# A fused attention and two-MoE kernel: blocks of four token tiles, a planner that models the VectorE/GpSimd port and two DMA rings, and new ranks

## The chip, the cores and the metric

One core of one Trainium2 chip runs the whole program. The metric is the device time of one execution in microseconds (us). The kernel before has a median of 745.53 us in three runs (744.16 to 746.38).

## The reference

Three layers follow each other, all in fp32.

- Clustered attention, batch 2, 8 heads, 768 tokens, head size 64. Queries and keys are assigned to the nearest of 16 centroids of their head (argmax of normalised products); a query sees only the keys of its own cluster: `scores = where(q_assign == k_assign, q @ k.T / 8, -1e9)`, softmax, `attn @ v`.
- First MoE layer on 1536 tokens of 512: `h = x @ w_in` (512 to 1024), `solu = h * softmax(h)`, layer norm over the 1024 with gain `g_ln`, `@ w_out` (1024 to 512).
- Second MoE layer: `((x @ w_a) * (x @ w_b)) @ w_out2`, 512 to 1536 to 512.

## The kernel before, in words

Every matmul operand is kept as two fp32r halves, `hi` (the rounded value) and `lo` (the rest), and a product is three matmuls (hi hi, hi lo, lo hi). ScalarE or GpSimd writes `hi` with a cast, VectorE or GpSimd writes `lo` with a subtraction. Weights arrive as 64-bit words of doubles; `weight()` turns each piece of 512 KB into fp32 with shifts and masks (lines 560 to 582) and then into two halves (591 and `sub`, 467 or 469).

Attention works on 8 pairs of heads. A pair is loaded and transposed (`qk_part`), compared with the centroids (`do_sim`, `do_sims`), turned into one-hot rows (`do_arg`, `do_oh`), and placed by DMA from SBUF to SBUF beside q and k (`do_place`, `do_ohd`), so that one extra matmul adds the mask. Then 96 steps of 128 queries follow: `score` (959), maximum (963), exp (967), `turn` (transposes 991, halves 1008 and 469), `apply` (1023 and after). The last part of `apply` writes the two halves of the layer's output into a common space of 12,288 columns, x.

The first MoE goes by 12 token tiles of 128: `moe_h` (1146), `moe_ln` (1163 to 1194), `moe_lnt` (1218), and, for each group of two tiles, `moe_x2` (1235, evictions 1249), which writes the new x in the place of the old.

The second MoE is cut into units. A unit is one block of token tiles and one of 12 slices of 128 hidden columns. `moe2_ab` multiplies the slice of `w_b` and of `w_a` with the block (1294, 12 matmuls each, the block's tokens as the moving columns), copies, multiplies and splits the result (1305 to 1308), and `moe2_y` multiplies it by the slice of `w_out2` (1322), three matmuls of 512 columns for each tile, adding up in PSUM over six slices. After the first six slices of a block the sum is put aside, after the last six it is added (1342) and sent out. A block has BT = 3 tiles, so BN = 384 moving columns, and there are 4 blocks. x is laid out by block: `[block][half][chunk of 128 inputs][384 tokens]`.

Nothing runs in the order in which it is written. `pl.add(engine, cost, rank, ...)` notes an operation with its buffers; `Plan.schedule` then simulates all engines, lets each take, of what is ready, the operation of the lowest rank, and emits the instructions in that order. Each engine then works in its order, held by semaphores. An operation's rank is a formula of its place plus corrections from the table `ADJ`, by kind, engine and number. SyncE issues all DMAs, and the planner gives a transfer a cost on one ring.

Of the kernel before, what the change touches and what calls it, by code (L numbers as in the profile page):

```python
# [33 lines left out]
ADJ = {  # L34
# [1374 lines left out]
```

## Time and profile before

| | us |
|---|---|
| median of three runs | 745.53 |
| the profiled execution | 743.77 |
| its span, first to last instruction | 742.0 |
| PE (TensorE matmul) busy | 711.1 |
| DVE (VectorE) busy | 473.7 |
| ACT (ScalarE) busy | 397.7 |
| POOL (GpSimd) busy | 339.5 |

The profile is of one execution. Engines are named as in the table; PEld is TensorE's weight load, which overlaps PE; SP is SyncE. Busy time counts instructions, not waiting, and the ends of matmuls are modelled. A group of instructions is shown with its line, engine, operation, `out<-in`, shapes and count. The chain of waits is followed back from the last instruction to what released it. Transfers moved 60.74 MB at a mean of 82 GB/s.

### The profile page before, as it was taken

The page shows a single profiled execution, that of the slowest core. Times are in us where ns is not written, and L with a number is a line of the kernel's source. Part 1 is how long each engine was busy: PE and PEld are TensorE (multiplying, and loading weights), DVE is VectorE, ACT ScalarE, POOL GpSimd, SP SyncE. Part 2 cuts the span into 40 slices and gives each one's busy share as a digit, 9 for nine tenths or more (in the row PEclk, how much of TensorE's full clock was granted, in tenths as well). Part 3 has the DMA queues.
Part 4 walks back from the last instruction along what each step waited for, and adds up shares of the span by engine and source line. Part 5 has one row for each costly group of instructions (what it writes and reads, how often), then busy time and mean ns, then how long its engine had stood idle before and what let it go on. Part 6 is the DMA issues. An engine that isn't in the chain of part 4 may idle for free.

```text
span 742.0 us, 12400 instructions
## 1 busy us (share of the span) xinstructions
PE 711.1 (96%) x4441; PEld 653.9 (88%) x4441; DVE 473.7 (64%) x866; ACT 397.7 (54%) x870; POOL 339.5 (46%) x429
## 2 busy tenths in 40 slices
PE   6889999999999999799999999999999999999997
PEld 6779888899999987678898999999999999999996
DVE  6899898988889878999688537763134311112122
ACT  4788899899899985564344424442224211211110
POOL 6568898857856425465515527771036300000000
PEclk9799999999999999999999999999999999999999
DMA  8878644454534001222301303431002000101011
GB/s 225 199 167 199 167 104 137 114 138 118 125 75 112 12 1 57 85 86 86 111 33 57 110 5 114 134 122 57 1 28 87 29 1 1 42 1 43 1 42 43
DMA packets 40573, 60.74 MB, mean 82 GB/s; under 512 B 3896, under 2 KB 35392, under 8 KB 40512
## 3 DMA queue, kind: packets, MB, share of 16 engines
q1 hardware_dynamic: 40512, 59.95, 29.0%
q8 instruction: 35, 0.57, 0.3%
q14 instruction: 26, 0.21, 0.1%
HBM read 36.74 MB, written 3.15 MB: 54 GB/s over the span
## 4 chain that ended last, share of the span: by engine, by line
PE 69%; DVE 18%; ACT 6%; issue 4%; POOL 2%; DMA 0%; DVEq 0%; ACTq 0%; POOLq 0%
PE psT L1294 12%; PE psS L1322 12%; PE psO L1023 6%; PE psM L1294 6%; PE psO L1294 6%; PE psT L991 6%; PE psS L959 6%; PE psS L1146 3%; PE psM L1235 3%; PE psO L1235 3%; DVE R L469 3%; DVE F L578 2%; DVE mxn L963 2%; DVE F L567 2%; ACT R L1008 1%
## 5 line engine op out<-in xcount | busy, mean ns | idle before, releaser
L469 DVE TENSOR_TENSOR R<-psT,R 128x384 fp32r<-128x384 f32 (+1 forms) x216 | 119.0, 565 | 26.9 <-ACT R L1008 23.3
L467 POOL TENSOR_TENSOR R<-F,R 128x512 fp32r<-128x512 f32 (+2 forms) x84 | 89.5, 1071 | 85.8 <-ACT R L591 81.7
L1294 PE MATMUL psT<-R 128*128 128x384 f32 x576 | 108.3, 337 | 0.0
L1322 PE MATMUL psS<-R 128*128 128x512 f32 x432 | 107.2, 393 | 0.2 <-ACT F L1340 0.2
L1294 PEld LDWEIGHTS psT<-R 128*128 128x128 f32 x576 | 102.1, 188 | 3.8
L991 PE MATMUL psT<-ident,F 128*128 128x128 f32 x576 | 92.8, 276 | 5.0 <-DVE R L469 4.4
L1008 ACT CAST R<-psT 128x384 fp32r<-128x384 f32 x192 | 90.1, 483 | 11.0 <-PE psT L991 8.8
L1322 PEld LDWEIGHTS psS<-R 128*128 128x128 f32 x432 | 80.2, 188 | 15.4 <-ACT F L1340 0.5
L1023 PE MATMUL psO<-R 128*128 128x256 f32 x576 | 91.0, 294 | 2.2 <-ACT F L1043 2.0
L959 PE MATMUL psS<-R 128*128 128x512 f32 (+3 forms) x384 | 92.2, 363 | 0.6 <-ACT F L967 0.6
L963 DVE TENSOR_REDUCE mxn<-psS 128x1 f32<-128x768 f32 x96 | 91.1, 948 | 2.0 <-PE psS L959 1.7
L967 ACT ACTIVATE F<-psS,mxn 128x768 f32<-128x768 f32 x96 | 87.5, 911 | 2.7 <-DVE mxn L963 2.4
L1307 ACT CAST R<-F 128x384 fp32r<-128x384 f32 x48 | 24.7, 515 | 102.6 <-PE psS L1322 100.6
L582 POOL TENSOR_TENSOR F<-F 128x512 int32<-128x512 int32 x45 | 60.2, 1339 | 41.6 <-DVE F L578 38.2
L1023 PEld LDWEIGHTS psO<-R 128*128 128x128 f32 x576 | 74.7, 189 | 4.1 <-ACT F L1043 3.3
L1308 DVE TENSOR_TENSOR R<-F,R 128x384 fp32r<-128x384 f32 x48 | 31.9, 664 | 70.6 <-ACT R L1307 70.5
L991 PEld LDWEIGHTS psT<-ident,F 128*128 128x128 f32 x576 | 66.5, 140 | 11.4 <-DVE R L469 8.0
L959 PEld LDWEIGHTS psS<-R 128*128 128x128 f32 (+1 forms) x384 | 66.8, 194 | 10.3 <-ACT F L967 1.5
L1146 PE MATMUL psS<-R 128*128 128x512 f32 x288 | 69.5, 394 | 1.5 <-DVE F L1167 1.2
L1146 PEld LDWEIGHTS psS<-R 128*128 128x128 f32 x288 | 52.9, 188 | 12.6 <-DVE F L1167 1.7
L1305 ACT COPY F<-psT 128x384 f32<-128x384 f32 x48 | 23.0, 479 | 60.5 <-PE psT L1294 59.5
L591 ACT CAST R<-F 128x512 fp32r<-128x512 f32 x52 | 32.2, 619 | 41.0 <-POOL F L582 33.2
(139 smaller groups left out, 1152.7 us busy)
## 6 DMA issues: line engine op xcount, KB each, us to landing
F<-in_moe_w_out_dram SPq DMA_DIRECT2D x20, 512.0 KB, 3.2
R<-R SPq DMA_DIRECT2D x32, 288.0 KB, 4.8
R<-R SPq DMA_DIRECT2D x32, 192.0 KB, 4.8
F<-in_moe_w_b_dram SPq DMA_DIRECT2D x12, 512.0 KB, 3.5
F<-in_moe_w_a_dram SPq DMA_DIRECT2D x12, 512.0 KB, 3.4
F<-in_moe_w_in_dram SPq DMA_DIRECT2D x8, 512.0 KB, 6.7
F<-in_v_dram SPq DMA_DIRECT2D x8, 384.0 KB, 3.3
R<-R SPq DMA_DIRECT2D x30, 96.0 KB, 2.7
```

Source lines behind the costliest of these rows:

```text
L467: pl.add("POOL", pool(n), rank, lambda: G.tensor_tensor(out=out_, in0=in0, in1=in1, op=ALU.subtract), reads, writes)
L469: pl.add("DVE", dve(n), rank, lambda: V.tensor_tensor(out=out_, in0=in0, in1=in1, op=ALU.subtract), reads, writes)
L582: pl.add("POOL", pool(n), rank, lambda: G.tensor_tensor(out=u, in0=u, in1=low, op=ALU.add), [rk, lwk], [uk])
L959: T.matmul(sp[:, c0:c0 + cn], kq[:r, 2 * m, t * P:(t + 1) * P], kq[:r, 2 * m + 1, c0:c0 + cn], start=m == 0, stop=m == 1)
L963: pl.add("DVE", dve(S), i + SUB["max"], lambda: V.tensor_reduce(out=mxn[:, b:b + 1], in_=sp[:, :S], axis=AX.X, op=ALU.max, negate=True), [ ...
L967: pl.add("ACT", act(S) + 93 + 93, i + SUB["exp"], lambda: A.activation(F[:, po:po + 768], sp[:, :S], AF.Exp, bias=mxn[:, b:b + 1], scale=1 ...
L991: T.transpose(sp[:, c, :], pt[:, kt * P:(kt + 1) * P], ident)
L1008: pl.add("ACT", act(HN), rk, lambda sp=sp, dh=dh: A.copy(dh, sp), [sk], [hk])
L1023: T.matmul(psO[:, :GN], vs[:, kt, j].rearrange("p l d -> p (l d)"), pt[:, m, kt, :], start=(kt == 0 and m == 0), stop=(kt == NT - 1 and m ...
L1146: T.matmul(sp[:, n0:n0 + 512], xb[:, a, c, ts_], winv[:, w, c, n0:n0 + 512], start=first, stop=(c == KD - 1 and a == 1))
L1294: T.matmul(pt[:, :BN], w[:, l, c, :], xb[:, a, c, :], start=first, stop=(c == KD - 1 and l == 1))
L1322: T.matmul(yv[t][0], hl2[a][:, ts_], wo[:, l, :], start=(first and a == 0 and l == 0), stop=(last and a == 1))
```

## The change

Five things change; the arithmetic does not.

- The planner's model. An operation can be marked `port=True` (VectorE steps that read and write SBUF with two ports); these and all GpSimd operations take turns at one port. A transfer is a pair of KB for two rings, each at 200 GB/s, and the ninth transfer waits for the first. `dma()` takes KB in place of nanoseconds; a plain transfer is split evenly, a placement goes by one ring.
- All ranks in `ADJ` have new values (669 entries are common to both tables, and none kept its value); `US`, the rank of a unit, goes from 2.45 to 3.27. What is done on which engine (`LO`), the formulas' other constants, and the 39 filling matmuls are as before.
- Blocks of the second MoE have four tiles: BT 4, BN 512, 3 blocks. x is laid out by tile: `[tile][half][chunk][128 tokens]`. So a moving operand of `moe2_ab` is four runs of 128, and a group of two tiles in `apply` and `moe_x2` is always one instruction where a block's edge split some before.
- The outputs go out tile by tile (12 transfers of 256 KB; before, three of 768 KB and three of 256 KB).
- Two GpSimd memsets and an exp of one column on ScalarE come first.

```diff
-    "apply0 0 PE": 12.667, "apply0 1 PE": -44.83, "apply0 2 PE": -56.922, "apply0 3 PE": -3.26,
...
+    "apply0 0 PE": -19.436, "apply0 1 PE": 133.47, "apply0 2 PE": 74.25, "apply0 3 PE": -29.828,
...
-    ISSUE, HEAD, TAIL, SLOW, DEPTH = 560.0, 950.0, 900.0, 1.6, 7000.0
+    ISSUE, HEAD, TAIL, LANES, RATE = 560.0, 1000.0, 800.0, 8, 200.0
...
+            if ops[i][6]:
+                s = max(s, port)
+                port = s + ops[i][1]
+            if eng == "SP":
+                s = max(s, lanes[0])
...
-                ring = max(ring, s + self.HEAD) + ops[i][1] * self.SLOW
-                free[eng] = max(s + self.ISSUE, ring - self.DEPTH)
-                end = ring + self.TAIL
+                free[eng] = s + self.ISSUE
+                end = 0.0
+                for h, kb in enumerate(ops[i][1]):
+                    if kb:
+                        ring[h] = max(ring[h], s + self.HEAD) + kb * 1e3 / self.RATE
+                        end = max(end, ring[h] + self.TAIL)
+                lanes = lanes[1:] + [end]
...
-    BT = NT // NB2
+    BT = 4
...
-        pl.add("SP", cost, rank, fn, reads, writes)
+        pl.add("SP", kb if isinstance(kb, tuple) else (kb / 2, kb / 2), rank, fn, reads, writes)
...
+    xv5 = R[:, X0:X0 + NTT * 1024].rearrange("p (t a c n) -> p t a c n", t=NTT, a=2, c=KD)
...
-            dma(1456, rank, lambda: Y.dma_start(view(ri), src), [], [rk, lwk])
+            dma(512, rank, lambda: Y.dma_start(view(ri), src), [], [rk, lwk])
...
+        pl.add("POOL", 100, Rk - 1, halves, [], ["half"])
+        pl.add("ACT", 1400, Rk, lambda: A.activation(one, half[:, 0:1], AF.Exp), ["half"], ["one"])
         pl.add("POOL", 480, Rk, lambda: make_identity(nc, ident), [], ["ident"])
...
+        copy("xhi", n * 3 + g, GN, rk, xv5[:, xs, 0, hp], src, [xk], [xk0])
+        sub("xlo", 0, GN, rk, xv5[:, xs, 1, hp], src, xv5[:, xs, 0, hp].bitcast(F32), [xk, xk0], [xk1], port=True)
...
-    US = 2.45
+    US = 3.27
...
-                        T.matmul(pt[:, :BN], w[:, l, c, :], xb[:, a, c, :],
+                        T.matmul(pt, w[:, l, c, :], xv5[:, xs, a, c, :],
...
-            pl.add("PE", mm_cost(DM, 9), rk, lambda: mm(range(BT)), rd, ["psS0", "psS1"])
+            pl.add("PE", mm_cost(DM, 3 * BT), rk, lambda: mm(range(BT)), rd, ["psS0", "psS1"])
...
-        if hf == 1 and not fin:
-            ov = F[:, oo:oo + 1536].rearrange("p (t d) -> p t d", t=BT)
-            dma(2184, rk, lambda: Y.dma_start(outv[b, g], ov), [fc((oo, 1536))], [])
+            if hf == 1:
+                b, r, a = (blk * BT + t) // NT, (blk * BT + t) % NT // HT, (blk * BT + t) % HT
+                dma(256, rk, lambda av=av, b=b, r=r, a=a: Y.dma_start(outv[b, r, a], av), [fk], [])
```

## Rows read from the trace of the kernel before

**Rows 1.** Stretches: length, busy PE, PEld, DVE, ACT, POOL (x instructions), clock, DMA share, GB/s.

```profile
0.00:60.00 60.00, 48.64 (x316) 42.84 (x317) 48.28 (x102) 41.23 (x93) 37.06 (x67) 0.91 0.78 193
60.00:285.00 225.00, 219.51 (x1605) 201.45 (x1604) 197.98 (x353) 205.73 (x493) 157.46 (x227) 1.00 0.42 107
285.00:450.00 165.00, 155.76 (x1014) 141.52 (x1015) 128.71 (x268) 77.21 (x143) 80.67 (x82) 1.00 0.22 74
450.00:700.00 250.00, 249.79 (x1321) 234.01 (x1320) 88.22 (x127) 68.07 (x132) 64.33 (x55) 1.00 0.14 45
700.00:742.00 42.00, 37.40 (x192) 34.04 (x190) 10.47 (x18) 5.49 (x11) 0.00 (x0) 0.97 0.10 38
```

**Rows 2.** Chain of waits in the second MoE: start us, us, engine, tile, line.

```profile
564.12 2.10 PE psT L1294 x12
566.23 2.08 PE psM L1294 x12
568.30 2.08 PE psS L1322 x9
570.39 2.10 PE psT L1294 x12
```

**Rows 3.** Shorter stretches of the opening, columns as in rows 1.

```profile
10.00:21.00 11.00, 5.32 (x36) 4.51 (x35) 10.04 (x26) 3.88 (x7) 6.99 (x8) 0.76 1.09 220
21.00:27.00 6.00, 5.71 (x26) 4.67 (x24) 3.85 (x8) 4.33 (x10) 2.56 (x2) 0.58 1.09 230
...
40.00:50.00 10.00, 6.97 (x49) 5.73 (x48) 9.88 (x18) 7.19 (x17) 5.83 (x5) 1.00 1.03 234
```

**Rows 4.** Timeline of DVE and of POOL, 13.9 to 21 us.

```profile
14.19 1.30 DVE L834 TENSOR_SCALAR F<-F 128x96 f32<-128x96 f32 x1
...
17.52 1.49 DVE L567 TENSOR_SCALAR F<-F 128x512 int32<-128x512 int32 x1
...
20.14 0.22 DVE L834 TENSOR_SCALAR F<-F 128x96 f32<-128x96 f32 x1
...
14.14 1.28 POOL L582 TENSOR_TENSOR F<-F 128x512 int32<-128x512 int32 x1 [1.18 <-DVE F L578]
...
17.45 1.27 POOL L467 TENSOR_TENSOR R<-F,R 128x512 fp32r<-128x512 f32 x1 [0.23 <-ACT R L591]
```

**Rows 5.** One line over the whole span: ns minimum/median/maximum, first and last start.

```profile
L567 DVE TENSOR_SCALAR F<-F x52: 404/464/1955, 12.5 to 582.2; 128x512 int32<-128x512 int32 x52
```

**Rows 6.** Chain of waits in the first MoE.

```profile
290.10 5.48 PE psS L1146 x24
```

**Rows 7.** Timeline of the end, from 731 us.

```profile
731.08 6.32 PE L1322 MATMUL psS<-R 128*128 128x512 f32 x27
...
733.13 0.51 ACT L1307 CAST R<-F 128x384 fp32r<-128x384 f32 x1 [3.40 <-PE psS L1322]
733.67 0.56 DVE L1308 TENSOR_TENSOR R<-F,R 128x384 fp32r<-128x384 f32 x1 [1.77 <-ACT R L1307]
736.76 1.89 DVE L1342 TENSOR_TENSOR F<-psS,F 128x512 f32<-128x512 f32 x3 [2.53 <-PE psS L1322]
```

**Rows 8.** Groups of ACT by shape: busy us, mean ns, idle before and its releasers.

```profile
L1249 ACT CAST R<-psO 128x256 fp32r<-128x256 f32 x8 | 3.0, 370 | 8.0 <-PE psO L1235 7.9
...
L1249 ACT CAST R<-psO 128x128 fp32r<-128x128 f32 x8 | 2.1, 268 | 5.3 <-PE psO L1235 3.6 <-DVE R L469 1.8
```

**Rows 9.** Timeline of ACT from the start.

```profile
0.72 1.28 ACT L723 ACT_TABLE_LOAD   x1 [0.72 <-PEq L1393]
...
5.05 0.49 ACT L723 ACTIVATE R<-psT 128x384 fp32r<-128x384 f32 x1 [3.05 <-PE psT L710]
```

**Rows 10.** Chain of waits in the opening.

```profile
12.58 0.65 DVE F L567
...
14.19 1.32 DVE F L834
...
17.61 1.40 DVE F L567
```

More of the change, by code (lines that the diff above doesn't have):

```diff
@@ new lines @@
+    "do_sims PE": -140.278, "do_v 0.0 POOL": 17.75, "do_v 0.1 POOL": -80.946, "do_v 1.0 POOL": 14.86,
+    "do_v 1.1 POOL": -6.61, "do_v 2.0 POOL": -43.216, "do_v 2.1 POOL": 3.463, "do_v 3.0 POOL": 26.005,
+    "do_v 3.1 POOL": -38.078, "do_v 4.0 POOL": 41.764, "do_v 4.1 POOL": 71.9, "do_v 5.1 POOL": -3.841,
+    "do_v 6.0 POOL": 48.143, "do_v 6.1 POOL": 1.505, "do_v 7.0 POOL": 17.899, "do_v POOL": 58.338,
+    "gains 0 DVE": -2.863, "gains 0 PE": 16.914, "gains DVE": -46.691, "gains PE": -125.86,
[42 rows of a table added]
@@ L239 @@
     WINDOW = 60.0
-    FIXED = ("ident", "iot", "cb", "g_sb")
+    FIXED = ("ident", "iot", "cb", "g_sb", "half")
     TICK = 10240 / 3
@@ L251, in __init__, with add @@
         self.keys = []
-    def add(self, eng, cost, rank, fn, reads=(), writes=(), after=0.0):
+    def add(self, eng, cost, rank, fn, reads=(), writes=(), after=0.0, port=False):
         me = len(self.ops)
@@ L276, in add @@
         self.keys.append(keys)
-        self.ops.append((eng, cost, rank + sum(ADJ.get(x, 0.0) for x in keys), fn, deps, after))
-    ISSUE, HEAD, TAIL, SLOW, DEPTH = 560.0, 950.0, 900.0, 1.6, 7000.0
+        self.ops.append((eng, cost, rank + sum(ADJ.get(x, 0.0) for x in keys), fn, deps, after, port or eng == "POOL"))
+    ISSUE, HEAD, TAIL, LANES, RATE = 560.0, 1000.0, 800.0, 8, 200.0
     def pe_end(self, cols, t, work):
@@ L303, in schedule @@
         free = {}
-        ring = 0.0
+        ring = [0.0, 0.0]
+        port = 0.0
+        lanes = [0.0] * self.LANES
         ready = {e: [] for e in self.ENGINES}
@@ L462, in on_pool, with sub @@
         return idx % mod in on
-    def sub(kind, idx, n, rank, out_, in0, in1, reads, writes):
+    def sub(kind, idx, n, rank, out_, in0, in1, reads, writes, port=False):
         if on_pool(kind, idx):
@@ L468, in sub @@
         else:
-            pl.add("DVE", dve(n), rank, lambda: V.tensor_tensor(out=out_, in0=in0, in1=in1, op=ALU.subtract), reads, writes)
+            pl.add("DVE", dve(n), rank, lambda: V.tensor_tensor(out=out_, in0=in0, in1=in1, op=ALU.subtract), reads, writes, port=port)
     def copy(kind, idx, n, rank, out_, in_, reads, writes):
@@ L477, in copy, with dma, xk_ @@
             pl.add("ACT", act(n, True), rank, lambda: A.copy(out_, in_), reads, writes)
-    def dma(cost, rank, fn, reads, writes):
-        pl.add("SP", cost, rank, fn, reads, writes)
-    def xoff(blk, a, c, t):
-        return X0 + blk * 3072 + a * 1536 + c * 384 + t * P
-    def xview(blk):
-        return R[:, X0 + blk * 3072:X0 + (blk + 1) * 3072].rearrange("p (a c n) -> p a c n", a=2, c=KD)
+    def dma(kb, rank, fn, reads, writes):
+        pl.add("SP", kb if isinstance(kb, tuple) else (kb / 2, kb / 2), rank, fn, reads, writes)
+    xv5 = R[:, X0:X0 + NTT * 1024].rearrange("p (t a c n) -> p t a c n", t=NTT, a=2, c=KD)
+    def xk_(ts, a, c):
+        return rc(*[(X0 + t * 1024 + a * 512 + c * P, P) for t in ts])
     ident = const.tile([P, P], F32, name="ident")
     half = const.tile([P, 2], F32, name="half")
+    one = const.tile([P, 1], F32, name="one")
     iot = const.tile([P, C], F32, name="iot")
@@ L646, in setup, with halves @@
         Rk = -200.0
+        def halves():
+            G.memset(half[:, 0:1], 0.5)
+            G.memset(half[:, 1:2], -0.5)
+        pl.add("POOL", 100, Rk - 1, halves, [], ["half"])
+        pl.add("ACT", 1400, Rk, lambda: A.activation(one, half[:, 0:1], AF.Exp), ["half"], ["one"])
         pl.add("POOL", 480, Rk, lambda: make_identity(nc, ident), [], ["ident"])
         def consts():
-            G.memset(half[:, 0:1], 0.5)
-            G.memset(half[:, 1:2], -0.5)
             for c in range(C):
@@ L666, in centroids @@
                 out=c_sq, in0=c_nat, scalar=1.0, in1=c_nat, op0=ALU.mult, op1=ALU.mult, accum_out=c_s[:, 0:1]), [cn], [ck, "c_s"]),
-            ("POOL", 470, lambda: G.tensor_tensor(out=c_s[:, 1:2], in0=c_s[:, 0:1], in1=half[:, 0:1], op=ALU.pow), ["iot"], ["c_s"]),
+            ("POOL", 470, lambda: G.tensor_tensor(out=c_s[:, 1:2], in0=c_s[:, 0:1], in1=half[:, 0:1], op=ALU.pow), ["half"], ["c_s"]),
             ("DVE", 70, lambda: V.tensor_scalar(out=c_s[:, 2:3], in0=c_s[:, 1:2], scalar1=1e-30, scalar2=None, op0=ALU.max), [], ["c_s"]),
@@ L733, in do_place @@
         kq, ko, hl = kqv(2 * n + j), kqo(2 * n + j), hlv(n)
-        rows, cost, d0, d1, s0, s1 = ((0, 275, 3, 4, 1, 2), (0, 820, 0, 3, 0, 3), (1, 546, 0, 2, 2, 4))[part]
+        rows, d0, d1, s0, s1 = ((0, 3, 4, 1, 2), (0, 0, 3, 0, 3), (1, 0, 2, 2, 4))[part]
         for r in range(2):
@@ L743, in do_place @@
             else:
-                dma(cost, rk, lambda dst=dst, src=src: Y.dma_start(dst.bitcast(F32), src.bitcast(F32)), rd, wr)
+                dma((0, 96 * (d1 - d0)) if rows else (96 * (d1 - d0), 0), rk, lambda dst=dst, src=src: Y.dma_start(dst.bitcast(F32), src.bitcast(F32)), rd, wr)
     def do_v(n, j, rk):
@@ L824, in do_arg @@
         if on_dve:
-            pl.add("DVE", dve(n_), rk, lambda: V.tensor_tensor(out=oh, in0=oh, in1=bc(m0), op=ALU.is_equal), [mk], sk)
-            pl.add("DVE", dve(n_), rk, lambda: V.tensor_tensor(out=oh, in0=oh, in1=io, op=ALU.mult), ["iot"], sk)
+            pl.add("DVE", dve(n_), rk, lambda: V.tensor_tensor(out=oh, in0=oh, in1=bc(m0), op=ALU.is_equal), [mk], sk, port=True)
+            pl.add("DVE", dve(n_), rk, lambda: V.tensor_tensor(out=oh, in0=oh, in1=io, op=ALU.mult), ["iot"], sk, port=True)
         else:
@@ L831, in do_arg @@
         if on_dve:
-            pl.add("DVE", dve(n_), rk, lambda: V.tensor_tensor(out=op, in0=oh, in1=bc(m1), op=ALU.is_equal), sk + [mk], ok)
+            pl.add("DVE", dve(n_), rk, lambda: V.tensor_tensor(out=op, in0=oh, in1=bc(m1), op=ALU.is_equal), sk + [mk], ok, port=True)
             if 1 in ss:
                 pl.add("DVE", dve2(n_ // len(ss)), rk, lambda: V.tensor_scalar(
-                    out=kop, in0=kop, scalar1=-1.0, scalar2=BIG, op0=ALU.add, op1=ALU.mult), [], kok)
+                    out=kop, in0=kop, scalar1=-1.0, scalar2=BIG, op0=ALU.add, op1=ALU.mult), [], kok, port=True)
         else:
@@ L1052, in apply @@
         pl.add("DVE", 72, i + 1, lambda: V.tensor_scalar(
-            out=rinv, in0=rsum[:, n % 2, g], scalar1=1e-9, scalar2=None, op0=ALU.add), [rm], ["rinv"])
+            out=rinv, in0=rsum[:, n % 2, g], scalar1=1e-9, scalar2=None, op0=ALU.add), [rm], ["rinv"], port=True)
         pl.add("DVE", 94, i + 1, lambda: V.reciprocal(out=rinv, in_=rinv), [], ["rinv"])
@@ L1074, in apply @@
                 out=xv, in0=xv, in1=psM[:, :GN], op=ALU.mult), ["psM"], [xk])
[L1075 to L1087 removed]
+        ts = range(b * NT + g * GT, b * NT + (g + 1) * GT)
+        xs = slice(ts[0], ts[-1] + 1)
+        src = xv.rearrange("p (t n) -> p t n", t=GT)
+        xk0, xk1 = xk_(ts, 0, hp), xk_(ts, 1, hp)
+        copy("xhi", n * 3 + g, GN, rk, xv5[:, xs, 0, hp], src, [xk], [xk0])
+        sub("xlo", 0, GN, rk, xv5[:, xs, 1, hp], src, xv5[:, xs, 0, hp].bitcast(F32), [xk, xk0], [xk1], port=True)
     winv = R[:, WIN_:WIN_ + 8192].rearrange("p (l c f) -> p l c f", l=2, c=KD)
@@ L1130, in load_wo1 @@
                gain=g_sb[:, f:f + 1], wg_off=WG_ + f % 2 * 512)
-    NTT = NBLK * BT
     NX2 = NTT // GT
     def moe_h(i):
-        blk, tt = i // BT, i % BT
-        xb = xview(blk)
-        ts_ = slice(tt * P, (tt + 1) * P)
         sp, sk = psS[i % 2], f"psS{i % 2}"
-        xk = [(xoff(blk, a, c, tt), P) for a in range(2) for c in range(KD)]
+        xk = [(X0 + i * 1024, 1024)]
         for n0 in range(0, F1, 512):
@@ L1187, in moe_ln @@
         ]
-        for eng, fn in seq:
-            pl.add(eng, 90 if eng == "DVE" else 470, rk, fn, [f"mv{b}"], [st])
+        for k, (eng, fn) in enumerate(seq):
+            two = k in (2, 5, 7, 8)
+            pl.add(eng, 90 if eng == "DVE" else 470, rk, fn, [f"mv{b}"], [st], port=two)
         if on_pool("lna", i):
@@ L1194, in moe_ln @@
             pl.add("DVE", 723, rk, lambda: V.tensor_scalar(
-                out=ln, in0=e, scalar1=s[:, 9:10], scalar2=s[:, 10:11], op0=ALU.mult, op1=ALU.add), [ek, st], [lk])
+                out=ln, in0=e, scalar1=s[:, 9:10], scalar2=s[:, 10:11], op0=ALU.mult, op1=ALU.add), [ek, st], [lk], port=True)
     def lnto(g, l, f, t=0):
@@ L1239, in moe_x2 @@
             pl.add("PE", mm_cost(GN, 12), rk, mm, [rc(*rd)], [sk])
-        i = g * GT
-        while i < (g + 1) * GT:
-            blk, tt = i // BT, i % BT
-            i1 = min((blk + 1) * BT, (g + 1) * GT)
-            w = (i1 - i) * P
-            xb = xview(blk)
-            src = sp[:, (i - g * GT) * P:(i1 - g * GT) * P]
-            cs = slice(tt * P, tt * P + w)
-            k0, k1 = (rc((xoff(blk, a, dm, tt), w)) for a in range(2))
-            pl.add("ACT", act(w), rk + 1, lambda xb=xb, src=src, cs=cs: A.copy(xb[:, 0, dm, cs], src), [sk], [k0])
-            sub("x2", g * KD + dm, w, rk + 1, xb[:, 1, dm, cs], src, xb[:, 0, dm, cs].bitcast(F32), [sk, k0], [k1])
-            i = i1
+        ts = range(g * GT, (g + 1) * GT)
+        xs = slice(ts[0], ts[-1] + 1)
+        src = sp[:, :GN].rearrange("p (t n) -> p t n", t=GT)
+        k0, k1 = xk_(ts, 0, dm), xk_(ts, 1, dm)
+        pl.add("ACT", act(GN), rk + 1, lambda: A.copy(xv5[:, xs, 0, dm], src), [sk], [k0])
+        sub("x2", g * KD + dm, GN, rk + 1, xv5[:, xs, 1, dm], src, xv5[:, xs, 0, dm].bitcast(F32), [sk, k0], [k1])
     HF = NF2 // 2
     T1 = T0 + NTT * TS + 5
-    US = 2.45
+    US = 3.27
     PIECES = [EW_ + i * 1024 for i in range(6)] + [WIN_ + i * 1024 for i in range(6)]
@@ L1276, in load_w2 @@
         weight(rank, src, shp, o, o + 512, RU[(f * 3 + x) % 2], "ACT", f * 3 + x)
-    outv = out.rearrange("(b p a r) d -> b r p a d", b=B, a=HT, r=2)
-    yv = [(psS[0][:, 0:512], "psS0"), (psS[0][:, 512:1024], "psS0"), (psS[1][:, 0:512], "psS1")]
+    outv = out.rearrange("(b p a r) d -> b r a p d", b=B, a=HT, r=2)
+    yv = [(psS[t // 2][:, t % 2 * 512:t % 2 * 512 + 512], (f"psS{t // 2}", 1 << t % 2)) for t in range(BT)]
     def moe2_ab(u, hf, blk, f):
-        xb = xview(blk)
+        xs = slice(blk * BT, (blk + 1) * BT)
         rk = T1 + u * US
@@ L1308, in moe2_ab @@
         pl.add("DVE", dve(BN), rk + 0.5, lambda: V.tensor_tensor(
-            out=lo, in0=bs, in1=hi.bitcast(F32), op=ALU.subtract), [bsk, h0], [h1])
+            out=lo, in0=bs, in1=hi.bitcast(F32), op=ALU.subtract), [bsk, h0], [h1], port=True)
     def moe2_y(u, hf, blk, f, first, last):
@@ L1333, in moe2_y @@
         span = blk == NBLK - 1
-        oo = OUT_ if span else ACC_ + blk * 1536
-        b, g = blk // NB2, blk % NB2
+        oo = OUT_ if span else ACC_ + blk * BN * KD
         for t in range(BT):
```

206 lines of the change are left out of this document (97 added, 109 removed), and 230 rows, old and new, of the table ADJ.

## The prediction

> **What bounds the kernel now.** I read the table of stretches first. It cuts the span of 742.0 us into opening, attention, first MoE, second MoE and tail, and the column to look at is PE's busy time beside the length of each stretch [rows 1]. In 450 to 700 us PE is busy 249.79 of 250 us: nothing but the number and the length of the matmuls matters there. Attention (60 to 285) leaves PE 225 - 219.51 = 5.5 us idle, the first MoE (285 to 450) 165 - 155.76 = 9.2, the opening (0 to 60) 60 - 48.64 = 11.4, the tail (700 to 742) 4.6. So there are two sources of gain: fewer or cheaper matmuls, and at most 5.5 + 9.2 + 11.4 = 26.1 us of idle time that another order could fill. A busy PE is modelled, so the true stalls may be somewhat longer.
>
> Then the chain of waits inside the second MoE: it is a strict period of 12 matmuls of 384 columns into psT, 12 into psO or psM, and 9 of 512 into psS, and psT returns after 570.39 - 564.12 = 6.27 us [rows 2]. No other engine stands in it.
>
> Then the opening at finer steps: from 10 to 21 us PE is busy 5.32 of 11 us while VectorE is busy 10.04, and the granted clock is 0.76; from 21 to 27 it is 0.58, a mix of the levels 2.4 and 1.2 GHz, after PE had been idle half of the 11 us before; from 40 to 50 PE is idle 3 us and VectorE busy 9.88 [rows 3]. So VectorE sets the opening. The timeline shows why it is slow: the mask step L834 takes 1.30 us where a later one of the same 96 elements takes 0.22, and it starts 0.05 us after a GpSimd addition of 1.28 us; L567 takes 1.49 us beside a GpSimd subtraction of 1.27 that began 0.07 us before [rows 4]. Over the program the 52 L567 go from 404 to 1955 ns (median 464) [rows 5]: the same instruction is long when it meets GpSimd.
>
> **The change, part by part.**
>
> Blocks of four tiles (BT 3 to 4). The second MoE goes from 4 blocks x 12 slices = 48 units to 3 x 12 = 36. A unit had 24 matmuls of 384 columns and 9 of 512; it has 24 of 512 and 12 of 512. The columns are the same; there are 48 x 24 - 36 x 24 = 288 fewer matmuls, and no fewer of the 512 into psS (432 both times). Before: 48 x 6.27 = 301.0 us. For 512 columns with a fresh stationary tile each the first MoE has 5.48 us for 24 [rows 6], and psS has 2.08 us for 9 [rows 2]. A new unit is 5.48 + 12 x 2.08 / 9 = 5.48 + 2.77 = 8.25 us, and 36 of them 297.0. Gain 4.0 us. If the new 512s ran at psS's 231 ns instead of 228, a unit would be 24 x 0.231 + 2.77 = 8.32 and the gain 1.5; if the period's other few hundredths also fell away with 12 units, 4.7. I take 4.0, the row nearest in kind. The evictions get a third longer, but their unit does too, and PE never waited for them. The ranks put a block's last matmuls one unit behind instead of two: the chain from psM to the two halves (multiply, cast, subtract) has 24 matmuls, 5.5 us, as cover; cast and subtract take 0.51 and 0.56 us at 384 columns [rows 7], so three steps of 512 with handovers come to some 2.4 us by estimate, and at the very end 2.77 us still hide them.
>
> What is this gain by the Trainium skill? "TensorE: Matmul & The Clock Gate", section Back-to-back issue gap, gives an isolated matmul its columns at 2.4 GHz plus 2.5 ns; by that 288 fewer would save 0.7 us. The trace disagrees: 2.10 us / 12 = 175 ns at 384 and 5.48 / 24 = 228 ns at 512 leave about 15 ns of fixed cost per matmul [rows 2, 6], and the rows decide; this case gets no chance of its own.
>
> The tail. The last unit sends four tiles instead of three. Its additions ran back to back, 1.89 us for three, the first beginning before the last matmul was through, and the transfers follow each [rows 7]. With four, two more additions have the two last tiles' matmuls as cover, so what follows the last matmul is the same: 0 (ends -0.6 and +0.6, one addition).
>
> Per-tile layout of x. Groups of two tiles no longer cross a block's edge, so 8 + 8 pairs of 128-wide evictions become 256-wide ones: 2 x 268 against 370 ns, 0.17 us less on ScalarE each [rows 8], and much the same on VectorE. That shortens how long psO and psM stay taken in the first MoE. I count it in the first MoE below.
>
> The exp table. One table load of 1.28 us stands at 0.72 us, and ScalarE's first real work comes at 5.05 us, with 3.05 us of idle between [rows 9]. There is no second load to save, and the added one-column exp fits in the gap: 0; if the gap were used, it would cost the load's 1.28 us at most. The two memsets moved ahead delay GpSimd's identity by 0.2 us, hidden by the same wait for the first transfers.
>
> The planner and all ranks. No instruction is added, but every engine's order is new, so this is bounded by the idle time and taken by place. Opening: on the chain stand L834 at 1.32 instead of 0.22 us (1.10 lost to GpSimd) and weight steps L567 of 0.65 and 1.40 that serve nobody so early [rows 10]. A planner that sees the lock would move these: 1.10 + 0.65 + 1.40 = 3.15 us; I take 2.5, since the weight steps must go somewhere in a VectorE that stays busy. Ends: 11.4 gained (all idle time) and 3.15 lost (the same bad luck once more). The clock: 5.71 us of PE time at 0.58 from 21 to 27 costs 2.4 us; a shorter wait may save it, a new one may add it; I take 0, ends -2.4 and +2.4. Attention: PE has 5.5 us idle; I take 1, ends 5.5 gained and 5.5 lost. First MoE: 9.2 idle, with VectorE busy 128.71 of 165; slower units (8.25 for 6.27) call for the second MoE's weights later, and the unsplit evictions help; I take 2.5, ends 9.2 gained and 6 lost, an estimate of two thirds of the same idle time.
>
> Sum: 4.0 + 2.5 + 0 + 1 + 2.5 = 10.0 us off the profiled execution's 743.77 (span 742.0 and 1.77 around it) is 733.8. The median of the runs is 745.53, 1.76 above that execution, so I forecast 735.5.
>
> **Rivals.**
>
> A: the new order gives nothing, and only the wider matmuls count: 745.53 - 4.0 = 741.5. For it: PE is busy 375.3 of the 390 us from 60 to 450 already, and the DMA engines' share is 1.09 from 10 to 21 us and 1.03 from 40 to 50 [rows 3], so a transfer and not the lock may end the opening. Against it: VectorE is as full there, with inflated instructions on the chain.
>
> B: the order does much better, half of the 26.1 us and the clock's 2.4 gone: 745.53 - 4.0 - 13 - 2.4 = 726. For it: the lock inflated VectorE everywhere (L567 up to four times its median).
>
> C, slower: the planner now thinks transfers too fast. It gives two rings 200 GB/s each, 400 together; the rows with a full share show 220 to 234 GB/s [rows 3], close to the old model's 512 KB in 1.456 x 1.6 us = 220. Loads of heads, placements and weights then land later than planned, engines that take their work in order stand behind them, PE idles and its clock falls. As much again as the opening's idle time, 11.4 us, plus 2.4 at the lower clock, with the matmuls' 4.0 kept: 745.53 - 4.0 + 13.8 = 755. It decides from 4.0 us of new waiting on. Against it: after 60 us the share is 0.42 and less [rows 1], so lateness only counts in the opening.
>
> D, slower: the moving operand is no longer one run. In moe2_ab 512 columns are now four runs of 128, 1024 apart. No matmul of this trace reads such an operand; if each of three breaks cost what a matmul's start costs, 15 ns, 864 x 45 ns = 39 us, 774 with all else as forecast; from 4.6 ns per matmul on the 4.0 us are lost. Against it: the runs are long. The Trainium skill ("Advanced Engine Details and Errata", Memory Cachelines) says that any non-contiguous pattern slows matmuls significantly, but says it of PSUM, which stays contiguous here; for SBUF it asks only that neighbours share a 16-byte line, which runs of 512 bytes do. No run here shows it yet.
>
> **How the numbers follow.** Forecast 0.48, A 0.22, B 0.14, C 0.12, D 0.04. A measurement here tells 0.3%, some 2.2 us, from no change. Faster gets 0.47 of the forecast, 0.16 of A, all of B and 0.01 of D (a loss under the gains): 0.78. Slower gets 0.11 of C and 0.03 of D: 0.14. The same gets the rest, mostly A with a little new waiting: 0.08. The range: B's 726 and somewhat beyond at one end, and at the other A with a little new waiting, 745; it leaves out C, D and the far part of B, about 0.2.
>
> **What would show it.** Right: psT returns every 8.25 us in the second MoE, 12 matmuls of 512 at 2.74 us; L834 near 0.3 us in the opening and PE's idle time before 60 us near 9; VectorE's L567 median-like in the mean; one table load. Wrong: 24 matmuls of psT and psO above 5.55 us (D); DMA waits ahead of PE, VectorE or ScalarE in the first 60 us (C); PE's idle time from 60 to 450 us above the 14.7 of before, or the opening no shorter (A).

## The result and the profile after

The changed kernel takes 735.39 us, median of four runs (734.1 to 738.21), against 745.51 for the kernel before beside it: a ratio of 0.9871 [0.9837, 0.9905]. I forecast 735.5: the forecast was 0.1 us off. The profiled execution took 734.58 us, with a span of 732.8.

The stretches of the changed kernel, to be laid beside [rows 1] (length, busy PE, PEld, DVE, ACT, POOL, clock, DMA share, GB/s):

```profile
0.00:60.00 60.00, 45.80 (x260) 40.63 (x260) 42.41 (x89) 34.17 (x75) 36.66 (x64) 0.80 0.70 173
60.00:285.00 225.00, 219.00 (x1620) 202.44 (x1621) 194.75 (x360) 207.58 (x502) 152.83 (x212) 1.00 0.44 110
285.00:450.00 165.00, 162.81 (x1048) 147.42 (x1046) 126.64 (x271) 84.75 (x148) 89.08 (x89) 1.00 0.25 81
450.00:700.00 250.00, 250.00 (x1108) 207.17 (x1107) 81.59 (x107) 65.10 (x110) 61.09 (x50) 1.00 0.14 45
```

Read the PE column. From 285 to 450 us PE idles 165 - 162.81 = 2.2 us where it idled 9.2. In the opening it idles 14.2 where it idled 11.4, and the granted clock fell to 0.80 there: the opening is worse, not better. The second MoE is as full as before, so its gain can only be in the matmuls. The chain of waits there, against [rows 2]:

```profile
562.31 2.72 PE psT L1298 x12
565.03 2.72 PE psO L1298 x12
567.75 2.72 PE psS L1326 x12
570.47 2.72 PE psT L1298 x12
```

psT returns after 570.47 - 562.31 = 8.16 us; I had 8.25. All 36 matmuls of a unit take 2.72 / 12 = 227 ns, whatever they read.

Idle time misses what the clock costs, so for the rest I use **lateness**: the start of the matmul issued last before a given time, counted from the start of the span, minus the matmul work issued up to there. A matmul counts at its full-clock length in the traces (226.5 ns for 512 columns, 173 for 384, 119 for 256, 108.5 for 128, 60 for fewer); the filling matmuls count nothing. This work is 676.0 us before and 672.4 after; with narrow blocks it is 676.0 too. The growth of lateness by stage, worked out from the matmul records of each profiled execution (the kernels e1 to e7 are explained below; before, a stall of 0.8 us straddles 285 us, so that row's two middle numbers are good to about half a us):

| kernel | to 100 us | 100 to 285 | 285 to 450 | 450 to the last matmul |
|---|---|---|---|---|
| before | 30.7 | 13.1 | 13.4 | 3.8 |
| after | 40.6 | 10.3 | 4.4 | 0.1 |
| e1, old planner, new blocks | 36.4 | 16.9 | 13.6 | 0.2 |
| e2, new planner, narrow blocks | 42.3 | 10.8 | 4.4 | 3.3 |
| e3, two instructions moved | 38.1 | 10.0 | 4.0 | 0.0 |
| e4, no exp first | 41.2 | 10.2 | 4.7 | 0.1 |
| e5, one queue | 33.2 | 13.9 | 3.6 | 0.0 |
| e6, one queue, second draw | 34.6 | 12.7 | 3.9 | 0.2 |
| e7, one queue, no port rule | 38.6 | 13.1 | 14.9 | 1.6 |

Each row is one execution, e1's the slowest of its ten and e3's the fastest of its four, so differences of a us or two between rows can be chance.

After against before: 9.9 us lost up to 100 us, then 2.8, 9.0 and 3.7 gained, and 3.6 less work. That is the 9.2 us by which the span is shorter. The total agrees with my forecast; its parts don't.

The 9.9 us have two sources of about the same size. Up to 100 us PE idles 18.4 us where it idled 12.9. And the granted clock is at 0.50, the lower of its two levels, for 3.4 + 20.5 = 23.9 us where it was there for 10.2 (first row before, the others after):

```profile
15.77:26.01 10.24, 6.87 (x28) 5.63 (x27) 7.47 (x18) 4.42 (x9) 5.21 (x5) 0.50 1.11 218
11.93:15.34 3.41, 3.41 (x18) 3.21 (x16) 3.41 (x11) 1.04 (x2) 2.77 (x4) 0.50 1.08 207
15.34:18.76 3.42, 1.46 (x10) 1.14 (x10) 3.23 (x6) 1.92 (x4) 1.39 (x1) 1.00 1.09 245
18.76:39.24 20.48, 14.99 (x62) 13.18 (x61) 14.72 (x27) 8.25 (x18) 7.36 (x8) 0.50 0.59 142
```

At half the clock half of the busy time is lost: by this estimate 6.87 / 2 = 3.4 us before and (3.41 + 14.99) / 2 = 9.2 after. That is 5.8 us more, beside 5.5 us more idle time. The long fall, at 18.8 us, follows a stretch in which PE was busy 1.46 of 3.4 us.

The lost part, in the chain of waits of the changed kernel's opening (start us, us, what; PEq and SPq are queues):

```profile
10.32 7.71 DMA R<-R
18.09 9.40 DMA F<-in_moe_w_in_dram
27.57 0.65 ACT F L576
...
29.92 0.90 PE psT L1011 x3
```

and in the timeline, ScalarE, GpSimd and PE behind it (in brackets: idle before, and what ended it):

```profile
18.09 0.35 SPq L574 DMA_DIRECT2D F<-in_moe_w_in_dram  x1
...
27.56 0.64 POOL L588 TENSOR_SCALAR F<-F 128x512 int32<-128x512 uint32 x1 [3.84 <-DMA F<-in_moe_w_in_dram]
27.57 0.65 ACT L576 ACTIVATE F<-F 128x512 f32<-128x512 f32 x1 [6.26 <-DMA F<-in_moe_w_in_dram]
...
29.92 0.90 PE L1011 MATMUL psT<-ident,F 128*128 128x128 f32 x3 [4.22 <-ACT F L987]
```

A piece of `w_in` is issued at 18.09 us and lands 9.4 us later. By the new planner's rule it would take 1.0 + 256 KB at 200 GB/s (1.28) + 0.8 = 3.1 us. So the planner put the piece's first two steps, on ScalarE (L576) and GpSimd (L588), ahead of attention's work. Both engines take their instructions in order; the exp of attention (L987) waits behind L576 and PE waits for the exp, 4.22 us. The clock is at 0.50 from 21 to 27 us and at 0.53 from 27 to 40:

```profile
21.00:27.00 6.00, 4.70 (x20) 4.11 (x18) 3.31 (x5) 0.32 (x2) 2.72 (x4) 0.50 1.05 203
27.00:40.00 13.00, 8.81 (x41) 7.67 (x41) 10.21 (x20) 8.02 (x17) 4.69 (x6) 0.53 0.26 81
```

The first of these rows also shows the resource: with the DMA engines fully taken (1.05) they move 203 GB/s, in [rows 3] 220 to 234. The new planner counts on 400; the old one, with 220 on one ring, was close. This is the mechanism of my rival C, in a kernel that is faster all the same.

### The profile page after: what moved, and what is told of

The parts are those of the page before. It is cut to its first block, busy times and chain, and to the rows that moved or that the text cites. A ratio compares the mean times of both kernels' runs of the same rounds, so it can differ in the third digit from the quotient of the medians.

```text
span 732.8 us, 11655 instructions
## 1 busy us (share of the span) xinstructions
PE 705.8 (96%) x4153; PEld 620.7 (85%) x4153; DVE 452.6 (62%) x833; ACT 395.2 (54%) x839; POOL 339.7 (46%) x413
## 4 chain that ended last, share of the span: by engine, by line
PE 83%; DMA 6%; ACT 3%; DVE 3%; POOL 2%; issue 2%; SPq 1%; DVEq 0%; ACTq 0%; POOLq 0%
PE psT L1298 13%; PE psS L1326 13%; PE psO L1043 8%; PE psS L979 8%; PE psT L1011 8%; PE psO L1298 7%; PE psM L1298 7%; PE psM L1245 5%; PE psS L1155 5%; PE psO L1245 5%; DMA F<-in_moe_w_in_dram 3%; PE psM L805 1%; PE psT L1228 1%; DMA R<-R 1%; PE psM L730 1%
## 5 line engine op out<-in xcount | busy, mean ns | idle before, releaser
L481 POOL TENSOR_TENSOR R<-F,R 128x512 fp32r<-128x512 f32 (+1 forms) x76 | 87.7, 1158 | 75.9 <-ACT R L607 73.8
L1298 PE MATMUL psT<-R 128*128 128x512 f32 x432 | 103.9, 389 | 0.0
L1326 PE MATMUL psS<-R 128*128 128x512 f32 x432 | 103.5, 389 | 0.0
L1011 PE MATMUL psT<-ident,F 128*128 128x128 f32 x576 | 91.0, 279 | 8.1 <-ACT F L987 6.7
L1298 PEld LDWEIGHTS psT<-R 128*128 128x128 f32 x432 | 80.9, 188 | 16.6
L987 ACT ACTIVATE F<-psS,mxn 128x768 f32<-128x768 f32 x96 | 87.5, 912 | 5.0 <-DVE mxn L983 4.5
L598 POOL TENSOR_TENSOR F<-F 128x512 int32<-128x512 int32 x45 | 62.0, 1379 | 34.0 <-DVE F L594 21.0
L979 PEld LDWEIGHTS psS<-R 128*128 128x128 f32 (+1 forms) x384 | 67.2, 195 | 11.4 <-issue 2.6
L1309 ACT COPY F<-psT 128x512 f32<-128x512 f32 x36 | 21.1, 587 | 102.7 <-PE psT L1298 102.7
L1155 PE MATMUL psS<-R 128*128 128x512 f32 x288 | 68.6, 393 | 1.9 <-DVE F L1176 1.9
L576 ACT ACTIVATE F<-F 128x512 f32<-128x512 f32 x48 | 32.6, 678 | 58.6 <-DMA F<-in_moe_w_out_dram 16.8
L1311 ACT CAST R<-F 128x512 fp32r<-128x512 f32 x36 | 22.3, 620 | 73.6 <-DVE F L1310 69.6
L1310 DVE TENSOR_TENSOR F<-psM,F 128x512 f32<-128x512 f32 x18 | 12.4, 691 | 77.9 <-PE psM L1298 77.8
```

The costliest lines, as they stand in the source:

```text
L481: pl.add("POOL", pool(n), rank, lambda: G.tensor_tensor(out=out_, in0=in0, in1=in1, op=ALU.subtract), reads, writes)
L979: T.matmul(sp[:, c0:c0 + cn], kq[:r, 2 * m, t * P:(t + 1) * P], kq[:r, 2 * m + 1, c0:c0 + cn], start=m == 0, stop=m == 1)
L987: pl.add("ACT", act(S) + 93 + 93, i + SUB["exp"], lambda: A.activation(F[:, po:po + 768], sp[:, :S], AF.Exp, bias=mxn[:, b:b + 1], scale=1 ...
L1011: T.transpose(sp[:, c, :], pt[:, kt * P:(kt + 1) * P], ident)
L1155: T.matmul(sp[:, n0:n0 + 512], xv5[:, i, a, c], winv[:, w, c, n0:n0 + 512], start=first, stop=(c == KD - 1 and a == 1))
L1298: T.matmul(pt, w[:, l, c, :], xv5[:, xs, a, c, :], start=first, stop=(c == KD - 1 and l == 1))
```

## The experiments

**e1: the old planner and ranks with the new blocks and layout.**

```diff
 # from the changed kernel; class Plan, ADJ, dma() and setup() as before the change
...
-                        ring[h] = max(ring[h], s + self.HEAD) + kb * 1e3 / self.RATE
...
+                ring = max(ring, s + self.HEAD) + ops[i][1] * self.SLOW
...
```

`US`, the rank step of a unit, stays at the changed kernel's 3.27.

> The kernel before with one part of the change: blocks of four tiles, x laid out by tile, outputs tile by tile. Planner, ranks and start as before. Width theory (the second MoE's period goes from 6.27 us x 48 to 8.16 x 36, as the changed kernel's trace has it): 7.2 us less, some 738.3; by the forecast's own term 4.0 less, 741.5. Rival (the change's gain lies in the order alone, width only shifts it): 743 or more. The period of psT tells width apart from anything that the old ranks do elsewhere: 8.16 by the first, 8.25 by the forecast.

Measured: 744.47 us, a ratio to the kernel before of 0.9985 [0.9966, 1.0003]. The chain in its second MoE:

```profile
563.13 2.72 PE psT L1280 x12
565.85 2.72 PE psM L1280 x12
568.57 2.72 PE psS L1308 x12
571.29 2.72 PE psT L1280 x12
```

The unit is the same 8.16 us, and by the table the second MoE keeps its gain (0.2 in place of 3.8, and 3.6 less work). The total is nevertheless in the rival's range, 743 or more: what the second MoE gains is lost elsewhere, 5.7 us more up to 100 us and 3.8 more up to 285. The execution profiled took 746.56 us (the ten go from 741.92), and the larger part of the 5.7 is its clock, at 0.50 for 20.5 of the first 100 us (by the estimate above 5.0 us more than before). That ranks made for the old blocks do worse with the new ones would explain the rest; no run shows it. The first MoE loses 13.6, as before: neither the unsplit evictions nor the layout help there.

**e2: the new planner and ranks with narrow blocks.**

```diff
-    BT = 4
+    BT = 3
...
-    US = 3.27
+    US = 2.45
...
```

> The changed kernel with blocks of three tiles again (384 columns, 48 units, rank step of a unit 2.45), x still laid out by tile, planner and ranks new. Up to the second MoE every engine has the changed kernel's order. Width theory: 48 x 6.27 against 36 x 8.16, so 7.2 us more than the changed kernel, 742.6. By the forecast's term 4.0 more, 739.4. Rival (the second MoE's tiles are refilled by other work, so width is worth little once the order is new): under 738. And the moving operand is then three runs of 128: if runs cost anything, the 12 matmuls of 384 columns take over 2.10 us; if not, 2.08 to 2.10 as before.

Measured: 744.73 us, ratio 0.9981 [0.9956, 1.0006]. Without its wide blocks the changed kernel is 744.73 - 735.39 = 9.3 us slower, more than twice what I had and 2 more than by the width theory; 6.8 of it stand in the second MoE (3.6 of work, 3.2 of lateness), the rest ahead of it and in what the runs scatter. The chain of its second MoE, where a block's operand is three runs of 128:

```profile
563.95 2.08 PE psS L1326 x9
566.03 2.10 PE psT L1298 x12
568.13 2.08 PE psM L1298 x12
```

A dozen of 384 columns takes 2.08 to 2.10 us, as in [rows 2], where it was one run. The gaps cost nothing that can be seen, and rival D is out. Without the wide blocks the rest of the change (planner, ranks, layout, outputs, start) is worth nothing that can be measured: in the table they gain 9.0 us in the first MoE and 2.3 in attention, and lose 11.6 ahead of it.

**e3: two instructions moved.** Only the two first steps of that one piece of `w_in` come later, behind what the plan starts by 25 us; the rest keeps its order.

```diff
-        for i in self.schedule():
+        order = self.schedule()
+        late = [i for i in order if self.ops[i][0] != "SP" and self.start[i] < 25000.0
+                and self.keys[i] and self.keys[i][1].startswith(('load_win 2 ',))]
+        rest = [i for i in order if i not in late]
+        at = sum(self.start[i] < 25000.0 for i in rest)
+        for i in rest[:at] + late + rest[at:]:
```

> The changed kernel with two instructions moved: ScalarE's and GpSimd's first step on the third piece of w_in stand some 10 places later in their queues (behind the first turns and scores). All other engines and the DMA queue keep their order. Head-of-line theory: ScalarE's 6.3 us wait for that transfer around 21 to 27.5 us holds up exp and the turns, PE idles 4.5 us and then runs at the low clock until about 40; without it PE's idle time before 60 us falls from 14.2 us by 4 or more, and the low clock ends at least 3 us sooner: 4 to 8 us less, 728 to 732. Rival (the opening is bound by the transfers themselves, whoever waits for them; the placements behind land as late): PE's idle time within 1 us, 734.5 to 736. Second rival (what is gained early is waited for later, at VectorE in attention): idle time before 60 falls, but the end moves by under 2 us.

Measured: 733.81 us, median of four runs (731.23, 733.25, 734.38, 742.54), ratio 0.9877 [0.9809, 0.9944]; the profiled execution is the first of these, with a span of 729.4, and its opening has PE busy 49.27 us, idle 10.7 instead of 14.2:

```profile
0.00:60.00 60.00, 49.27 (x289) 44.08 (x290) 45.72 (x97) 37.21 (x83) 37.99 (x66) 0.83 0.72 189
```

The stall is where the trace says: PE's idle time up to 100 us falls from 18.4 to 14.5 us. But the time falls by 1.6 us by the medians (2.1 without the last run), not by 4 to 8, and the intervals don't tell that from nothing; the lateness at 100 us falls by 2.5. The long stretch at the low clock ends 2.6 us sooner, at 36.6 us, and another of 3.4 us follows at 77.6, so PE spends 23.9 us at 0.50 as in the changed kernel. One stall is not the opening.

**e4: no exp ahead.**

```diff
-        pl.add("ACT", 1400, Rk, lambda: A.activation(one, half[:, 0:1], AF.Exp), ["half"], ["one"])
```

> The changed kernel without the one-column exp at the start; all other instructions in the same order on every engine. By the forecast's term (one table load of 1.28 us, hidden in ScalarE's first idle time) no change, 735.4 within 0.3%. Rival (the exp pulls the load of the right table ahead, and without it a second load appears or the first one comes late): a second table load in the trace or one in front of the first cast, 1.3 us or more on top, 736.7.

Measured: 735.76 us, ratio 0.9866 [0.9839, 0.9893]: with or without it the same. In the changed kernel the load is one, as before, and as long as in [rows 9]:

```profile
0.72 1.28 ACT L668 ACT_TABLE_LOAD   x1 [0.72 <-PEq L1394]
2.01 0.20 ACT L668 ACTIVATE one<-half 128x1 f32<-128x1 f32 x1
4.69 0.49 ACT L737 ACTIVATE F<-psT 128x384 f32<-128x384 f32 x1 [2.48 <-PE psT L730]
```

In e4 there is one load as well, but it comes late and stands in front of the first cast, as the rival had it:

```profile
3.86 1.28 ACT L737 ACT_TABLE_LOAD   x1 [3.86 <-DMA F<-in_k_dram]
5.15 0.49 ACT L737 ACTIVATE F<-psT 128x384 f32<-128x384 f32 x1
```

The cast starts 0.46 us later for it, not 1.3, and the time doesn't show that.

**e5 and e6: one queue in the planner.** I took the issue times that the changed kernel's trace has for its transfers of the first 100 us and asked each model when the 67 of known landing should land. Two rings of 200 GB/s are 1.8 us early in the mean, 5.6 at worst, 2.5 in root mean square. One queue in order, 230 GB/s for loads and 200 for copies from SBUF to SBUF, is off by 0.1 in the mean and 0.6 in root mean square. The Trainium skill ("DMA: Bandwidth & Descriptors", Queues, rings and completion order) gives SP one row of rings, one on each of the 16 DMA engines; by that there is no second ring on which a transfer could pass, and the fit agrees in the times, though the page says too that completion is not strictly in order. The planner of before had one ring too (512 KB in 1.456 x 1.6 = 2.33 us, 220 GB/s), and on the same transfers it is off by 0.1 in the mean and 0.6 in root mean square: the change replaced a good model of the transfers by a worse one. So the planner got one queue, and the corrections in `ADJ` were searched again against it, in two independent draws.

```diff
-                for h, kb in enumerate(ops[i][1]):
-                    if kb:
-                        ring[h] = max(ring[h], s + self.HEAD) + kb * 1e3 / self.RATE
-                        end = max(end, ring[h] + self.TAIL)
+                ring = max(ring, s + self.HEAD) + ops[i][1]
+                end = ring + self.TAIL
...
+        pl.add("SP", (sum(kb) if isinstance(kb, tuple) else kb) * 1e3 / (200 if place else 230), rank, fn, reads, writes)
```

> The changed kernel, its planner's two rings of 200 GB/s each replaced by one queue for all transfers (230 GB/s for loads, 200 GB/s for the copies from SBUF to SBUF), and the rank corrections searched anew for that; port rule, widths, layout and exponential unchanged. The planned end is 721.5 us; the order of the changed kernel, replayed with the one queue, ends at 740.1 (measured: a span of 732.8). Theory: the two rings made the changed kernel issue instructions too early for their data in the first 100 us, where it runs 10 us later than the kernel before, and an order that knows the one queue gets that back: 722 us (716 to 728), lateness at 100 us at or under 31 (changed kernel 40.6, kernel before 30.7). Rival: a planner's model shifts stalls and gains nothing: 733 us or more, and the stalls return in later stages.

> As the run before, with another, independent draw of the search for the rank corrections (planned end 722.9 us). If the planner's transfer model is what counts, it is within 5 us of the first draw, around 723 us; if a single good draw is what counts, the two differ by more than that, and this one may stand at 733 us.

Measured: e5 730.35 us, 0.9798 [0.9777, 0.9818]; e6 731.72, 0.9812 [0.9791, 0.9833]. Both beat both kernels, and they agree within 1.4 us. That is 5.0 and 3.7 us under the changed kernel, about a third of the 13 I expected, and outside my 716 to 728: lateness at 100 us fell by 7.4 and 6.0 of the 9.9 lost (33.2, not the 31 expected), and attention after it gave 2.4 to 3.6 back. The opening of e5:

```profile
10.00:21.00 11.00, 6.11 (x37) 5.17 (x37) 8.93 (x22) 4.50 (x9) 7.57 (x8) 0.78 0.99 247
21.00:27.00 6.00, 6.00 (x26) 5.25 (x25) 5.40 (x13) 2.60 (x6) 3.82 (x6) 0.54 1.06 259
27.00:40.00 13.00, 10.67 (x71) 8.62 (x70) 11.31 (x20) 11.00 (x25) 4.78 (x6) 1.00 0.47 145
```

From 27 to 40 us PE is at full clock and issues 71 matmuls, the changed kernel 41. From 21 to 27 the DMA engines are as full (share 1.06, 259 GB/s); what changed is the work that stands behind them. What PE waits for in the first 100 us (us in total, times, longest) shows that too, first of the changed kernel, then of e5:

```profile
PE psT L1011 <- ACT F L987: 6.7, 4, 4.2
```

```profile
PE psM L786 <- DVE R L747: 2.7, 1, 2.7
PE psS L979 <- ACT F L987: 2.7, 3, 1.5
...
PE psT L1011 <- ACT F L987: 0.2, 1, 0.2
```

What the other engines wait for shows the cause. In the changed kernel ScalarE waits for pieces of `w_in` in the first 100 us (as above):

```profile
ACT F L576 <- DMA F<-in_moe_w_in_dram: 12.1, 4, 6.3
```

and GpSimd 10.2 us more. These waits of the two engines add up to 22.3 us in the changed kernel and 19.2, 10.3 and 23.0 in e2, e3 and e4, which have its planner. In the kernels whose planners know one ring or queue they are 1.4 in e1 and 0.6 in e7, and none is listed before and in e5 and e6.

Model and search change together here, and no kernel was searched anew under the two rings and run. That the waits for `w_in` go with the two rings is shown; that a new search alone would have given some of e5's gain is not excluded.

**e7: one queue, no port rule.** As e5, but GpSimd and VectorE never wait for each other in the plan, and ranks searched without the rule.

```diff
-        self.ops.append((eng, cost, rank + sum(ADJ.get(x, 0.0) for x in keys), fn, deps, after, port or eng == "POOL"))
+        self.ops.append((eng, cost, rank + sum(ADJ.get(x, 0.0) for x in keys), fn, deps, after, False))
```

> One queue as in the two runs before, but the planner's rule that VectorE's two-input instructions and GpSimd's hold one port in turn is taken out, and the ranks searched anew without it. The planned end is 712.7 us; the same order replayed with the rule ends at 748.1 us. If the rule describes the chip, this kernel is far slower than its plan: 735 to 748 us, with VectorE or GpSimd instructions stretched at more places than in the first of these runs. If the instructions run beside each other at nearly full speed, it is 712 to 722 us and the fastest here.

Measured: 747.83 us, 1.0035 [1.0021, 1.0048]. Its span is 745.5 us where its own plan says 712.7 and the plan replayed with the rule 748.1, and it takes 17.5 us more than e5. By the table most of it is lost in the first MoE (14.9 against 3.6), some up to 100 us (38.6 against 33.2). So with one queue but without the port rule the opening is only 2.0 us better than the changed kernel's, which points to e5 needing both; it is one draw of the search. PE's wait for the exp in the first 100 us is back too (6.3 us, at most 2.1 at a time), with next to no waiting for `w_in`, so that wait alone is no sign of late transfers. VectorE and GpSimd in the first MoE:

```profile
343.18 1.25 DVE L1184 SCALAR_TENSOR_TENSOR stt<-mv,stt 128x1 f32<-128x1 f32 x1
...
348.01 1.16 DVE L1188 SCALAR_TENSOR_TENSOR stt<-stt 128x1 f32<-128x1 f32 x1
...
351.21 1.22 DVE L1184 SCALAR_TENSOR_TENSOR stt<-mv,stt 128x1 f32<-128x1 f32 x1
```

```profile
342.85 1.56 POOL L481 TENSOR_TENSOR R<-F,R 128x512 fp32r<-128x512 f32 x1 [2.31 <-ACT R L607]
...
347.87 1.29 POOL L481 TENSOR_TENSOR R<-F,R 128x512 fp32r<-128x512 f32 x1
...
351.10 1.31 POOL L598 TENSOR_TENSOR F<-F 128x512 int32<-128x512 int32 x1 [1.94 <-DVE F L594]
```

An instruction on one element per partition takes 1.25 us and ends at 344.43; the GpSimd instruction beside it ends at 344.41. The next pairs end at 349.17 and 349.16, 352.43 and 352.41. At its shortest the first of these lines takes 203 ns. The Trainium skill ("SBUF — State Buffer", SBUF: two separate sides) calls the pair of ports that the two engines share an exclusive lock, held for a whole instruction, also against a VectorE instruction with two SBUF inputs; these three pairs agree. PE pays for it in this kernel's first MoE (waits, as above):

```profile
PE psS L1155 <- DVE F L1176: 3.9, 4, 1.7
PE psM L1245 <- DVE R L483: 2.0, 2, 1.2
PE psS L1155 <- DVE stt L1190: 1.3, 1, 1.3
```

where the kernel before has 9.4 us of such waits in its list, the largest of them

```profile
PE psT L1218 <- ACT F L588: 2.4, 1, 2.4
PE psM L1235 <- DVE R L469: 2.3, 3, 1.2
```

and the changed kernel 2.2:

```profile
PE psS L1155 <- DVE F L1176: 1.9, 2, 1.6
PE psT L1228 <- ACT F L1201: 0.3, 1, 0.3
```

## Why the prediction was right, and where its parts were not

**Blocks of four, -4.0: right in kind, too small.** The period is 8.16 us and not 8.25, which makes 36 x 8.16 = 293.8 against 301.0: 7.2 us. The term that I mis-sized is the 512-column matmul: I took 228 and 231 ns from [rows 6] and from the nine of [rows 2], and it is 227 in all matmuls of the new unit. Over 36 units, 24 matmuls at 1.6 ns less and 12 at 4.4 less are 1.4 + 1.9 us, within rounding the missing 3.2. My upper end, 4.7, was too tight. The rows of before were not misread: in its matmul records, and in e2's, the nine of psS do follow each other at 231 ns in the mean, and the first five of the next dozen at 175 to 185 where the others take 173. In the new unit, with 512 columns throughout, all are 227 apart. Why the mixed unit is slower is not shown.

**Opening, -2.5: wrong in sign.** It lost 9.9 us up to 100 us. I counted what the lock costs there and gave 0.12 to the transfers being planned too early. The lock is still there (L854, the L834 of before, takes 0.97 us once and L845 1.27 in the changed kernel's opening, each ending 0.1 us behind a GpSimd instruction), and rival C's mechanism is what happened: SP's transfers late, work of attention behind them, PE idle, low clock, at 9.9 in place of my 13.8. My sign for C, DMA waits ahead of ScalarE in the first 60 us, is there. Against C's terms the idle time is smaller, 5.5 and not 11.4, and the clock larger, 5.8 and not 2.4. In e5 and e6, planned with one queue, 7.4 and 6.0 of the 9.9 come back. Nothing in the sum stood for the case that a gain elsewhere could hide it: I had made C a rival for the whole, with the 4.0 us as the only gain against it.

**First MoE, -2.5: 9.0, and it goes with the port rule.** I thought of unsplit evictions and a fuller order. e1 has the evictions and loses 13.6 us there; every kernel with the port rule loses 3.6 to 4.7, and e7, with ranks searched without the rule, 14.9. The rule does not make the lock rare: VectorE's time above the shortest of each form, from 285 to 450 us, is 28.5 us before, 23.6 after, 26.3 in e5 and 27.8 in e7, summed over its records. e5 has only 2.2 us less of it than the kernel before, and 9.8 us less lateness. A plan that knows when VectorE will be late can put the work that PE needs ahead of the rest; that would explain it, and no run shows this step by itself.

**Attention, -1: 2.8.** Within its bounds; no run isolates it. **Clock, 0:** wrong. By the estimate above it cost 5.8 us more than before, outside my ends of 2.4 either way; it is included in the 9.9. **Tail, 0:** right; from the start of the last matmul to the end it is 4.98 us before and 4.93 after. Four additions, the first two under matmuls:

```profile
722.62 5.60 PE L1326 MATMUL psS<-R 128*128 128x512 f32 x24
...
726.90 2.65 DVE L1345 TENSOR_TENSOR F<-psS,F 128x512 f32<-128x512 f32 x4 [1.94 <-PE psS L1326]
```

**Exp first, 0:** right. **D:** false; the Trainium skill, "Advanced Engine Details and Errata", Memory Cachelines, asks of SBUF only neighbours within a line, and the rows of e2 agree, 2.08 us for twelve in one run or in three.

**In sum** I expected 2.5 + 1 + 2.5 = 6.0 from the order and 4.0 from the blocks. The order gave 2.8 + 9.0 - 9.9 = 1.9 and the blocks with their stalls 3.6 + 3.7 = 7.3. Together that is 9.2 us by the profiled executions and 10.1 by the medians, where I had 10.0. That the forecast is 0.1 us off is luck: an error of 12.4 us in the opening stood against 6.5, 3.3 and 1.8 in the first MoE, the second and attention. B and C both came true in part, in different stages. Nor do the two halves of the change add up: the blocks without the order (e1) and the order without the blocks (e2) gain about 1 us each, not clear of noise, and both together 10.1.

## What to carry to other kernels

Where a planner writes the order, its model of a resource can decide the outcome (e7 lost 17.5 us with one rule left out): check it against the trace, resource by resource, by feeding it the traced issue times and comparing when it thinks that things end. Forecast such a change stage by stage, and let a harmful model cost its place even where the total gains. For a matmul's length at a new shape take the longest undisturbed run of that shape, since a few nanoseconds times a thousand matmuls are the size of the gain.

## What was not expected of the hardware

- Transfers that SP issues behave as one queue (67 landings fit it within 0.6 us in root mean square): with the DMA engines' share near one, 203 to 271 GB/s in the stretches read here (271 in e5, from 16.2 to 26.5 us), far from the 400 of two rings; the median from issue to landing is 5.9 us for the eight 512 KB pieces of `w_in` (issued from 3.9 to 108.3 us) and 3.2 for the twenty of `w_out`.
- The lock's price is the rest of GpSimd's instruction, not VectorE's own length: 128x1 elements took 1.25 us in e7. By the sum of such stretches in the first MoE (28.5 us of VectorE before, 26.3 in e5) most of the gain there came without fewer collisions.
- A moving operand of three or four runs of 128 fp32r elements streams like one run (2.08 us for twelve matmuls of 384 columns in e2, and 227 ns for 512 in the changed kernel, as for the one run of psS).
